# Three edits to a fused attention and gated-FFN kernel: row transposes on the DMA, a swapped subtraction, and a nested product in the paired FFN blocks

## The chip, the cores and the metric

The kernel runs on one core of one Trainium2 chip. The metric is device time in microseconds (us) from launch to end. A core has five engines with a queue each: TensorE (PE, matrix products), VectorE (DVE), ScalarE (ACT), GpSimd (POOL) and SyncE (SP, which here issues most DMAs). Each engine works through its own queue in order and waits for others by semaphores. TensorE writes its results to PSUM, which has eight banks of 128 x 512 fp32 values.

## The reference

```python
h  = x + _A_ref(_layernorm(x), wqkv, wo)      # x: 1 x 2048 x 1024, bf16
h2 = h + _B_ref(_layernorm(h), w_gate, w_up, w_down)

def _A_ref(x, wqkv, wo):      # 32 heads of 32, each position looks at itself
    ...                       # and 7 earlier ones, 2 apart
    return softmax-weighted values @ wo

def _B_ref(x, w_gate, w_up, w_down):          # F = 3584
    g = jnp.einsum("bsd,df->bsf", x, w_gate)
    u = jnp.einsum("bsd,df->bsf", x, w_up)
    return jnp.einsum("bsf,fd->bsd", g * u, w_down)
```

Both layer norms have mean and variance over 1024 values, without weights.

## The kernel before, in words

The 2048 rows are worked on in four chunks of 512 (0 to 3). A chunk's rows are normalized and transposed, so that `lnT` holds 8 slices of 128 features by 512 rows. Projections follow, in groups of eight matmuls of 512 columns that fill a PSUM bank (line 489); then attention on VectorE, the output projection `wo`, a second normalization, and the FFN. All instructions are emitted in a schedule written by hand: each engine executes its part in the order in which the program emits it. A `Background` object slips VectorE and ScalarE work (attention, normalization) in between the groups, according to a budget in us that the generators state with `yield`.

*Chunk 1's first normalization.* `rows_gen` (lines 249 to 262) emits, for four row tiles of 128 rows, statistics (`stat`), the normalized rows (`norm`, line 195) and the transpose. Tiles 0 and 1 are transposed on TensorE (line 245: eight 128 x 128 transposes a tile, into two PSUM banks) and copied to `lnT` by ScalarE and VectorE (line 247). Tiles 2 and 3 are transposed by a DMA issued from ScalarE's queue (line 236). Chunk 2 uses the same generator without transposes. Chunk 1's tile is first multiplied after the twelve groups of chunk 0's blocks 1 to 3. SyncE's queue meanwhile stores queries (line 395) and keys and values (line 415), and loads weights (line 172) and rows (line 209).

*The FFN of chunks 0 and 1* is done group by group. *Chunks 2 and 3* are worked on together, with sums in the manner of Strassen and Winograd: a product of 2 x 2 blocks takes seven block products instead of eight. Here the two halves of the 1024 features and the two chunks make the activation blocks `b11` to `b22`; two halves of a weight tile of 256 columns and two halves of the features make the weight blocks. `activation_sums` (line 835) makes the differences `t1` to `t4` once. There are 14 blocks (`NP`), each for 256 columns of both `w_gate` (i = 0) and `w_up` (i = 1). `weight_sums(n)` scales block n's weights to fp16 (line 823, VectorE) and makes four sums of 128 x 512 for gate and for up (lines 828 to 831), on VectorE for block 0 and on GpSimd for the others; it is emitted at the start of block n-1, so it runs while TensorE works on block n-1. GpSimd does gate's four sums first, then up's.

`pair_block(n)` (line 850) has fourteen products of four matmuls of 512 columns (line 847, `product`), seven for gate and seven for up, in banks x, y, z and v. A partial result is copied from bank to bank by ScalarE (lines 864 and 872) and further products are added to the copy. The fifth product of each (bank v, `sw[:, i, 0]` by `t1`) goes to SBUF scaled, as `p5` (line 869), and is added by VectorE to two of the four outputs (lines 875 and 884). Outputs of gate and up are then multiplied (line 886). Earlier outputs are summed by their absolute values on ScalarE (line 369, `sums`). PSUM tiles share one pool of eight buffers, and a block uses eight.

*Chunk 1's down projection* runs before the paired blocks, likewise in seven products (`dprod`, line 1108; `t_half`, line 1101, for differences of the weights; `put`, line 805, for results). Its last part is interleaved with the second normalization of chunk 3: after `rstd_of` on ScalarE, VectorE forms the bias `nbs[3]` (line 1351), which ScalarE uses for the rows (`ln_rows`, line 1197). Line 1352 and line 1354 form `t4` in two halves, from `b21` (loaded and converted before) and `t2`.

Of the kernel before, what the change touches and what calls it, by code (L numbers as in the profile page):

```python
# [25 lines left out]
TC = 512  # L26
NCH = S // TC
SUB = TC // 4
KO = D // 128
NF = F // 128  # L30
NP = NF // 2
# [47 lines left out]
def kernel(  # L79
# [11 lines left out]
    nc = tc.nc  # L91
    x = A_x.flatten_outer_dims()
# [7 lines left out]
    lnTp = ctx.enter_context(tc.tile_pool(name="lnT", bufs=3))  # L100
# [4 lines left out]
    att = ctx.enter_context(tc.tile_pool(name="att", bufs=1))  # L105
    psum = ctx.enter_context(tc.tile_pool(name="psum", bufs=8, space=PSUM))
# [106 lines left out]
    lnTs = {}  # L213
# [3 lines left out]
    class Norm1:  # L217
# [11 lines left out]
        def norm(self, t):  # L229
            self.lns[t] = normalize(xtiles[self.c][t], self.mv4, self.rs4, t)  # L230

        def transpose(self, t, eng=nc.sync):
            c = self.c
            if c not in lnTs:
                lnTs[c] = lnTp.tile([128, KO, TC], BF, tag="lnT", name=f"lnT1_{c}")
            eng.dma_start_transpose(lnTs[c][:, :, bass.ts(t, 128)], self.lns[t][:])

        def transpose_on_array(self, t):
            c = self.c
            if c not in lnTs:  # L240
                lnTs[c] = lnTp.tile([128, KO, TC], BF, tag="lnT", name=f"lnT1_{c}")
            for hf in range(2):
                pt = psum.tile([128, KO // 2, 128], BF, tag="mm", name=f"ptb{c}_{t}_{hf}")
                for kk in range(KO // 2):
                    nc.tensor.transpose(pt[:, kk, :], self.lns[t][:, bass.ts(4 * hf + kk, 128)], ident[:])
                copy = nc.vector.tensor_copy if hf else nc.scalar.copy
                copy(lnTs[c][:, bass.ts(hf, 4), bass.ts(t, 128)], pt[:])

    def rows_gen(n, on_array):
        for t in range(6):  # L250
            if t < 4:
                n.stat(t)
                yield 1.5
            if 0 < t < 5:
                n.norm(t - 1)
                yield 0.55
            if t > 1 and on_array:
                if t < 4:
                    n.transpose_on_array(t - 2)
                    yield 0.45  # L260
                else:
                    n.transpose(t - 2, nc.scalar)

    class NormOnScalar(Norm1):

# [80 lines left out]
    ident = const.tile([128, 128], BF)  # L346
# [131 lines left out]
    xtiles[2] = load_x(2, "x", nc.sync)  # L478
    norm1 = {1: Norm1(1), 2: Norm1(2), 3: NormOnScalar(3)}
    bg.add(rows_gen(norm1[1], True))  # L480
    rows2 = rows_gen(norm1[2], False)
    bg.add(rows2)
    for j in range(4):
# [324 lines left out]
    pair = {}  # L808
# [8 lines left out]
    def weight_sums(n, eng=nc.gpsimd):  # L817
        raw = pair["w", n]
        wt = wpool.tile([128, KO, 2, 256], F16, tag="w", name=f"ws_{n}")
        if n == 0:  # L820
            nc.scalar.activation(wt[:], raw[:], ACTF.Copy, scale=scale_gu.s)
        else:
            nc.vector.tensor_scalar(wt[:], raw[:], scale_gu.s, None, ALU.mult)
        sw = wpool.tile([128, 2, 4, 4, 128], F16, tag="w", name=f"sw_{n}")
        for i in ((slice(0, 2),) if eng is nc.vector else (slice(0, 1), slice(1, 2))):
            a11, a21, a12, a22 = (wt[:, k:k + 4, i, c:c + 128].rearrange("p k i c -> p i k c")
                                  for k in (0, 4) for c in (0, 128))
            eng.tensor_tensor(sw[:, i, 0], a21, a22, ALU.add)  # L828
            eng.tensor_tensor(sw[:, i, 1], sw[:, i, 0], a11, ALU.subtract)  # L829
            eng.tensor_tensor(sw[:, i, 2], a11, a21, ALU.subtract)  # L830
            eng.tensor_tensor(sw[:, i, 3], a12, sw[:, i, 1], ALU.subtract)  # L831
        pair["a", n], pair["s", n] = wt, sw
        state["live"] += 1

# [10 lines left out]
    def product(ps, lhs, rhs, fresh):  # L845
        for ko in range(4):
            nc.tensor.matmul(ps[:], lhsT=lhs[:, ko, :], rhs=rhs[:, ko, :], start=(fresh and ko == 0),  # L847
                             stop=(ko == 3), skip_group_check=not fresh)

    def pair_block(n, hts, sums=()):  # L850
        b11, b21, t1, t2, t3, t4, b22 = pair["b"]
        wt, sw, inv = pair["a", n], pair["s", n], scale_gu.inv
        gu = range(2)
        out = [hts, [t1k.tile([128, TC], BF, tag="t1k", name=f"up{n}_{k}")[:] for k in range(4)]]

        def bank(k, i):
            return psum.tile([128, TC], F32, tag="mm", name=f"p{k}{n}_{i}")

        xb, yb, zb, vb, p5 = [[None] * 2 for _ in range(5)]
        for i in gu:  # L860
            xb[i] = bank("x", i)
            product(xb[i], wt[:, 0:4, i, 0:128], b11, True)
            yb[i] = bank("y", i)
            nc.scalar.copy(yb[i][:], xb[i][:])  # L864
        for i in gu:
            vb[i] = bank("v", i)
            product(vb[i], sw[:, i, 0], t1, True)
            p5[i] = att.tile([128, TC], F32, tag=("lg", "t3")[i], name=f"p5{n}_{i}")
            nc.scalar.activation(p5[i][:], vb[i][:], ACTF.Copy, scale=inv)
            product(yb[i], sw[:, i, 1], t2, False)  # L870
            zb[i] = bank("z", i)
            nc.scalar.copy(zb[i][:], yb[i][:])
        for i in gu:
            product(zb[i], sw[:, i, 2], t3, False)
            nc.vector.scalar_tensor_tensor(out[i][3], zb[i][:], inv, p5[i][:], ALU.mult, ALU.add)
            product(xb[i], wt[:, 4:8, i, 0:128], b21, False)
            nc.scalar.activation(out[i][0], xb[i][:], ACTF.Copy, scale=inv)
            for k in sums[2 * i:2 * i + 2]:
                k()
        for i in gu:  # L880
            product(zb[i], wt[:, 4:8, i, 128:256], t4, False)
            nc.scalar.activation(out[i][2], zb[i][:], ACTF.Copy, scale=inv)
            product(yb[i], sw[:, i, 3], b22, False)
            nc.vector.scalar_tensor_tensor(out[i][1], yb[i][:], inv, p5[i][:], ALU.mult, ALU.add)
        for k in (3, 0, 2, 1):
            nc.vector.tensor_tensor(out[0][k], out[0][k], out[1][k], ALU.mult)
        state["live"] -= 2
# [211 lines left out]
    def sub(dst, x0, x1, eng=nc.vector):  # L1099
        for d, a0, a1 in zip(dst, x0, x1):  # L1100
            eng.tensor_tensor(f16(d[:, 0:NH, :]), f16(a0[:, 0:NH, :]), f16(a1[:, 0:NH, :]), ALU.subtract)
# [25 lines left out]
    b11, b21 = ([wts["dn", n, a] for a in range(2)] for n in ("11", "21"))  # L1127

    def halves(parts, name):
        return [pool.tile([128, KO, TC], BF, tag=tag, name=f"{name}{i}") for i, (pool, tag) in enumerate(parts)]  # L1130

    b12 = halves(((att, "qD"), (att, "kD")), "b12")
    a21 = halves(((lnTp, "lnT"), (lnTp, "lnT")), "a21")
    a22 = halves(((lnTp, "lnT"), (wpool, "w")), "a22")
# [33 lines left out]
    def ln_stat(c, t):  # L1168
        stats(hss[c][t], ln2[c][0], t)
# [42 lines left out]
    def t_half(dst, x0, x1, a):  # L1212
        sub([dst[a]], [x0[a]], [x1[a]])
# [42 lines left out]
    b22 = halves(((lnTp, "lnT"), (wpool, "w")), "b22")  # L1256
# [15 lines left out]
    t2 = halves(((wpool, "w"), (wpool, "w")), "t2_")  # L1272
# [16 lines left out]
    room = wpool.tile([128, 4, TC], F32, tag="w", name="hsr0")  # L1289
# [4 lines left out]
    b21 = halves(((lnTp, "lnT"), (lnTp, "lnT")), "b21r")  # L1294
# [10 lines left out]
    a22 = halves(((att, "vD"), (att, "oD")), "a22r")  # L1305
# [42 lines left out]
    t4 = t2  # L1348
    ln_stat(3, 3)
    rstd_of(ln2[3][0], ln2[3][1], 0, 4)  # L1350
    nc.vector.scalar_tensor_tensor(nbs[3], ln2[3][0][:, :, 0], -1.0, ln2[3][1][:], ALU.mult, ALU.mult)
    t_half(t4, b21, t2, 0)
    l3 = lnTp.tile([128, KO, TC], BF, tag="lnT", name="lnT2_3")
    t_half(t4, b21, t2, 1)
    for q in range(4):
# [4 lines left out]
    retire(2)  # L1360
    load_pair(1)
    weight_sums(0, nc.vector)
    for q in range(4):
        dprod(zs[q], q, F22, fcells(t4), False)
# [153 lines left out]
```

## Time and profile before

| | |
|---|---|
| median of 10 runs | 767.84 us (767.62 to 768.65) |
| the profiled execution | 768.01 us, span of its instructions 765.9 us |
| granted TensorE clock | 1.000 |
| matmul instructions | 3648 |
| matmuls of the paired blocks (line 847) | 784 of 512 columns |
| line 836 to 842, `activation_sums` | four VectorE operations of 1.2 us |
| DMA | 145.77 MB, mean 190 GB/s |

The span runs from the first to the last instruction; the time of an execution has some 2 us around it. In lines of operations the columns are: start in us, duration in us, engine, line, operation, tile written <- tiles read, shapes, count, and in brackets how long the engine had been idle before and what ended that. In rows of a line's statistics, three durations are the shortest, the median and the longest in ns. Rows of several operations ("x3") give the time from the first start to the last end. The row of a stretch gives its bounds, its length, and the busy us of PE, the weight loads (PEld), DVE, ACT and POOL, each with a number of instructions, then the clock, the DMA share and GB/s. A wait row gives total us, number of times, and the longest.

### The profile page before, as it was taken

Reading aid. Unit: us, or ns where it says so; the run is one execution under the profiler, and the core shown is the slowest. Engines: PE = TensorE matmul, PEld = TensorE weight load, DVE = VectorE, ACT = ScalarE, POOL = GpSimd, SP = SyncE. Lnnn points to the kernel's source line nnn. Section 1 sums busy time; section 2 is a strip of 40 time slices with the busy share of each in tenths; the row PEclk is TensorE's granted clock in tenths of the full one; section 3 lists DMA queues with packets and bytes.
Section 4 is the critical chain, followed back from the end, with each engine's and each line's share of the span. In section 5 each row is a group of like instructions: output and inputs, shape, how many; then the busy total and the mean of one; then the engine's idle time right before and its main releaser. Section 6 shows DMA issues by size and latency. Waiting matters only on the chain.

```text
span 765.9 us, 10355 instructions
## 1 busy us (share of the span) xinstructions
PE 759.6 (99%) x3648; PEld 349.3 (46%) x3648; DVE 627.8 (82%) x760; ACT 532.9 (70%) x1012; POOL 144.7 (19%) x155
## 2 busy tenths in 40 slices
PE   8999999999999999999999999999999999999998
PEld 5444444444444444444444444444444444444444
DVE  6789999999999999999999999976554454578862
ACT  4757854556799598996898984846767677788230
POOL 0010000200001000010000001018778777600000
PEclk9999999999999999999999999999999999999999
DMA  8889794968998959869768528684242432830001
GB/s 270 232 236 262 183 288 106 321 176 193 326 342 285 312 168 316 259 229 339 251 213 280 171 92 285 147 203 127 63 110 58 108 90 76 269 117 27 1 28 55
DMA packets 191987, 145.77 MB, mean 190 GB/s; under 512 B 81856, under 2 KB 182080, under 8 KB 189888
## 3 DMA queue, kind: packets, MB, share of 16 engines
q1 hardware_dynamic: 180416, 116.94, 53.6%
q0 software_dynamic: 3728, 22.02, 8.4%
q10 hardware_dynamic: 7792, 6.16, 2.7%
q8 instruction: 28, 0.46, 0.3%
q14 instruction: 23, 0.19, 0.1%
HBM read 111.02 MB, written 27.26 MB: 181 GB/s over the span
## 4 chain that ended last, share of the span: by engine, by line
PE 86%; DVE 5%; ACT 5%; DMA 3%; issue 0%; SPq 0%; ACTq 0%; DVEq 0%
PE ps L489 17%; PE dx L1108 6%; PE py L847 6%; PE px L847 6%; PE pwg L489 6%; PE pz L847 6%; PE pwu L489 6%; PE pu L489 6%; PE pg L489 6%; PE wo L661 4%; PE pv L847 3%; PE dy L1108 3%; PE wo L1162 2%; DMA b21r<-in_B_w_down_dram 2%; PE ez L1108 2%; ACT gs L1087 1%
## 5 line engine op out<-in xcount | busy, mean ns | idle before, releaser
L489 PE MATMUL ps<-lnT,w_qkv 128*128 128x512 bf16 x608 | 132.1, 379 | 0.0
L489 PEld LDWEIGHTS <-w_qkv 128*128 128x128 bf16 (+1 forms) x608 | 59.3, 98 | 70.9
L546 DVE TENSOR_TENSOR prod<-qD,kD 128x4096 bf16<-128x4096 bf16 (+1 forms) x34 | 72.2, 2158 | 2.2 <-DMA kD<-kd 2.2
L594 DVE TENSOR_TENSOR pv<-vD,at 128x4096 bf16<-128x4096 bf16 x32 | 72.4, 2286 | 0.3
L847 PEld LDWEIGHTS <-sw 128*128 128x128 f16 x448 | 43.8, 98 | 52.9 <-issue 0.2
L489 PEld LDWEIGHTS <-w_wg 128*128 128x128 bf16 x448 | 43.8, 98 | 52.8
L489 PEld LDWEIGHTS <-w_wu 128*128 128x128 bf16 x448 | 43.8, 98 | 52.9
L403 ACT CAST sg<-ps 128x512 bf16<-128x512 f32 x72 | 41.5, 584 | 31.9 <-PE ps L489 27.3
L847 PE MATMUL px<-lnT,ws 128*128 128x512 bf16 x224 | 55.2, 379 | 0.0
L489 PE MATMUL pg<-lnT,w_wg 128*128 128x512 bf16 x224 | 52.9, 379 | 0.0
L489 PE MATMUL pu<-lnT,w_wu 128*128 128x512 bf16 x224 | 52.9, 379 | 0.0
L489 PE MATMUL pwu<-lnT,w_wu 128*128 128x512 bf16 x224 | 52.9, 379 | 0.0
L489 PE MATMUL pwg<-lnT,w_wg 128*128 128x512 bf16 x224 | 52.9, 379 | 0.0
L847 PEld LDWEIGHTS <-ws 128*128 128x128 f16 x336 | 32.9, 98 | 39.7
L607 POOL DMA_DIRECT2D od<-oD x4 | 2.2, 542 | 250.1 <-DVE oD L605 250.1
L828 POOL TENSOR_TENSOR sw<-ws 128x512 f16<-128x512 f16 x26 | 30.0, 1153 | 79.0 <-PE pz L847 47.4
L1108 PEld LDWEIGHTS <-gs 128*128 128x128 f16 (+1 forms) x280 | 27.3, 98 | 33.1 <-DVE gs L1276 0.5
L548 DVE TENSOR_TENSOR prod<-prod 128x4096 bf16<-128x4096 bf16 x16 | 36.6, 2286 | 0.3
L864 ACT COPY py<-px 128x512 f32<-128x512 f32 x28 | 16.0, 570 | 24.4 <-PE px L847 24.4
L831 POOL TENSOR_TENSOR sw<-ws,sw 128x512 f16<-128x512 f16 x26 | 30.6, 1175 | 0.0
L829 POOL TENSOR_TENSOR sw<-sw,ws 128x512 f16<-128x512 f16 x26 | 30.0, 1153 | 2.0
L830 POOL TENSOR_TENSOR sw<-ws 128x512 f16<-128x512 f16 x26 | 30.2, 1160 | 0.0
(371 smaller groups left out, 1577.8 us busy)
## 6 DMA issues: line engine op xcount, KB each, us to landing
w_wg<-in_B_w_gate_dram SPq DMA_DIRECT2D x14, 1024.0 KB, 7.5
w_wu<-in_B_w_up_dram SPq DMA_DIRECT2D x14, 1024.0 KB, 9.3
w_pair<-in_B_w_gate_dram SPq DMA_DIRECT2D x14, 512.0 KB, 4.0
w_pair<-in_B_w_up_dram SPq DMA_DIRECT2D x14, 512.0 KB, 5.3
w_wo<-in_A_wo_dram SPq DMA_DIRECT2D x6, 1024.0 KB, 8.3
w_qkv<-in_A_wqkv_dram SPq DMA_DIRECT2D x5, 1024.0 KB, 9.3
kd<-sg SPq DMA_DIRECT2D x32, 144.0 KB, 4.2
vd<-sg SPq DMA_DIRECT2D x32, 144.0 KB, 3.2
```

The costliest lines, as they stand in the source:

```text
L403: nc.scalar.copy(sg[:, HB:HB + TC], ps[:])
L489: nc.tensor.matmul(ps[:], lhsT=wt[:, ko, bass.ts(j, 128)], rhs=rhs[:, ko, :], start=(ko == 0), stop=(ko == KO - 1))
L546: nc.vector.tensor_tensor(prod[:, j, ds], qD[:, ds], kD[:, ds, o:o + SUB], ALU.mult)
L548: nc.vector.tensor_tensor(prod[:, :, 0:16], prod[:, :, 0:16], prod[:, :, 16:32], ALU.add)
L594: nc.vector.tensor_tensor(pv[:, j], vD[:, :, o:o + SUB], at[:, w, None, :].to_broadcast((128, DH, SUB)), ALU.mult)
L661: nc.tensor.matmul(ps[:], lhsT=oTs[c][:, kk, t, :], rhs=wts["wo", c, hf][:, kk, :], start=(kk == 0), stop=(kk == KO - 1))
L828: eng.tensor_tensor(sw[:, i, 0], a21, a22, ALU.add)
L829: eng.tensor_tensor(sw[:, i, 1], sw[:, i, 0], a11, ALU.subtract)
L830: eng.tensor_tensor(sw[:, i, 2], a11, a21, ALU.subtract)
L831: eng.tensor_tensor(sw[:, i, 3], a12, sw[:, i, 1], ALU.subtract)
L847: nc.tensor.matmul(ps[:], lhsT=lhs[:, ko, :], rhs=rhs[:, ko, :], start=(fresh and ko == 0), stop=(ko == 3), skip_group_check=not fresh)
L1108: nc.tensor.matmul(ps[:, bass.ds(lo, n)], lhsT=lhs[k][:, bass.ts(q, 128)], rhs=rhs[k][:, bass.ds(lo, n)], start=(fresh and k == 0), stop=( ...
```

## The change

Chunk 1: all four row tiles are transposed by DMA from SyncE's queue; the method that used TensorE is gone, with its copies and the 0.45 that the generator charged for each.

```diff
-        def transpose(self, t, eng=nc.sync):
+        def transpose(self, t):
...
-            eng.dma_start_transpose(lnTs[c][:, :, bass.ts(t, 128)], self.lns[t][:])
-
-        def transpose_on_array(self, t):
...
+            nc.sync.dma_start_transpose(lnTs[c][:, :, bass.ts(t, 128)], self.lns[t][:])
...
-            if t > 1 and on_array:
-                if t < 4:
-                    n.transpose_on_array(t - 2)
-                    yield 0.45
-                else:
-                    n.transpose(t - 2, nc.scalar)
+            if t > 1 and turned:
+                n.transpose(t - 2)
```

Chunk 1's down weights: the first half of `t4` is emitted ahead of the bias.

```diff
     rstd_of(ln2[3][0], ln2[3][1], 0, 4)
+    t_half(t4, b21, t2, 0)
     nc.vector.scalar_tensor_tensor(nbs[3], ln2[3][0][:, :, 0], -1.0, ln2[3][1][:], ALU.mult, ALU.mult)
-    t_half(t4, b21, t2, 0)
```

The paired blocks: in blocks 1 to 13 the two fifth products (gate's and up's, together 256 columns of weights by 512 features by 512 values of `t1`) are taken as one product of 2 x 2 blocks and done again in seven smaller products, `inner`, each two matmuls of 256 columns. Two banks, `first` and `last`, take the place of the two banks v. `inner_rows` makes the differences of `t1` once, in block 0; `inner_weights(n + 1)` makes the weights' sums in every block but the last, on VectorE between the two operations of line 884. GpSimd's sums are emitted one kind at a time, for gate and up, in place of all kinds for gate and then for up.

```diff
-        for i in ((slice(0, 2),) if eng is nc.vector else (slice(0, 1), slice(1, 2))):
...
+        for j, x, y, op in ((0, a21, a22, ALU.add), (1, sw[:, :, 0], a11, ALU.subtract), (2, a11, a21, ALU.subtract),
+                            (3, a12, sw[:, :, 1], ALU.subtract)):
+            for i in each:
+                eng.tensor_tensor(sw[:, i, j], x[:, i], y[:, i], op)
...
+    def inner_rows(t):
+        room = att.tile([128, KO, TC], F16, tag="vD", name="inner_t")
+        b11, b12, b21, b22 = (t[:, k:k + 2, c:c + 256] for k in (0, 2) for c in (0, 256))
+        t1, t2, t3, t4 = (room[:, i, :].rearrange("p (k c) -> p k c", k=2) for i in range(4))
+        nc.vector.tensor_tensor(t1, b12, b11, ALU.subtract)
+        nc.vector.tensor_tensor(t2, b22, t1, ALU.subtract)
+        nc.vector.tensor_tensor(t3, b22, b12, ALU.subtract)
+        nc.vector.tensor_tensor(t4, b21, t2, ALU.subtract)
+        pair["iv"] = room[:, 4, :].bitcast(F32)
+        pair["ib"] = (b11, b21, t1, t2, t3, t4, b22)
+
+    def inner_weights(n):
+        sw = pair["s", n]
+        a11, a12, a21, a22 = (sw[:, i, 0, k:k + 2, :] for i in range(2) for k in (0, 2))
+        room = att.tile([128, 4, 2, 128], F16, tag="at", name=f"inner_w{n}")
+        s1, s2, s3, s4 = (room[:, i] for i in range(4))
+        nc.vector.tensor_tensor(s1, a21, a22, ALU.add)
+        nc.vector.tensor_tensor(s2, s1, a11, ALU.subtract)
+        nc.vector.tensor_tensor(s3, a11, a21, ALU.subtract)
+        nc.vector.tensor_tensor(s4, a12, s2, ALU.subtract)
+        pair["ia", n] = (a11, a12, a22, s1, s2, s3, s4)
+
+    def inner(ps, lhs, rhs, fresh):
+        for k in range(2):
+            nc.tensor.matmul(ps, lhsT=lhs[:, k, :], rhs=rhs[:, k, :], start=(fresh and k == 0), stop=(k == 1),
+                             skip_group_check=not fresh)
...
+            first, last = bank("i", 0), bank("i", 1)
+            lx, lv = (first[:, bass.ts(i, 256)] for i in range(2))
+            ly, lz = (last[:, bass.ts(i, 256)] for i in range(2))
+            v5 = pair["iv"]
         for i in gu:
...
             nc.scalar.copy(yb[i][:], xb[i][:])
+            if nested and i == 0:
+                inner(lx, a11, c11, True)
+                inner(lv, s1, r1, False)
+                nc.scalar.activation(v5, lv, ACTF.Copy, scale=inv)
+                nc.scalar.copy(ly, lx)
         for i in gu:
-            vb[i] = bank("v", i)
-            product(vb[i], sw[:, i, 0], t1, True)
...
+            if not nested:
+                vb[i] = bank("v", i)
+                product(vb[i], sw[:, i, 0], t1, True)
+                nc.scalar.activation(p5[i][:], vb[i][:], ACTF.Copy, scale=inv)
             product(yb[i], sw[:, i, 1], t2, False)
...
+            if nested and i == 0:
+                inner(ly, s2, r2, False)
+                inner(lx, a12, c21, False)
+                nc.scalar.copy(lz, ly)
+                nc.scalar.activation(p5[0][:, 0:256], lx, ACTF.Copy, scale=inv)
+        if nested:
+            inner(lz, s3, r3, False)
+            inner(ly, s4, c22, False)
+            nc.vector.scalar_tensor_tensor(p5[0][:, 256:512], ly, inv, v5, ALU.mult, ALU.add)
+            nc.vector.scalar_tensor_tensor(p5[1][:, 256:512], lz, inv, v5, ALU.mult, ALU.add)
         for i in gu:
...
             nc.scalar.activation(out[i][0], xb[i][:], ACTF.Copy, scale=inv)
+            if nested and i == 0:
+                inner(lz, a22, r4, False)
+                nc.scalar.activation(p5[1][:, 0:256], lz, ACTF.Copy, scale=inv)
...
             nc.vector.scalar_tensor_tensor(out[i][1], yb[i][:], inv, p5[i][:], ALU.mult, ALU.add)
+            if i == 0 and n + 1 < NP:
+                if n == 0:
+                    inner_rows(t1)
+                inner_weights(n + 1)
```

More of the change, by code (lines that the diff above doesn't have):

```diff
@@ L235, in transpose, with rows_gen @@
                 lnTs[c] = lnTp.tile([128, KO, TC], BF, tag="lnT", name=f"lnT1_{c}")
-            eng.dma_start_transpose(lnTs[c][:, :, bass.ts(t, 128)], self.lns[t][:])
-        def transpose_on_array(self, t):
[L239 to L249, printed above, removed]
+            nc.sync.dma_start_transpose(lnTs[c][:, :, bass.ts(t, 128)], self.lns[t][:])
+    def rows_gen(n, turned):
         for t in range(6):
@@ L824, in weight_sums @@
         sw = wpool.tile([128, 2, 4, 4, 128], F16, tag="w", name=f"sw_{n}")
-        for i in ((slice(0, 2),) if eng is nc.vector else (slice(0, 1), slice(1, 2))):
[L826 to L831, printed above, removed]
+        a11, a21, a12, a22 = (wt[:, k:k + 4, :, c:c + 128].rearrange("p k i c -> p i k c")
+                              for k in (0, 4) for c in (0, 128))
+        both = (slice(0, 2),)
+        each = both if eng is nc.vector else (slice(0, 1), slice(1, 2))
+        for j, x, y, op in ((0, a21, a22, ALU.add), (1, sw[:, :, 0], a11, ALU.subtract), (2, a11, a21, ALU.subtract),
+                            (3, a12, sw[:, :, 1], ALU.subtract)):
+            for i in each:
+                eng.tensor_tensor(sw[:, i, j], x[:, i], y[:, i], op)
         pair["a", n], pair["s", n] = wt, sw
@@ L859, in pair_block @@
         xb, yb, zb, vb, p5 = [[None] * 2 for _ in range(5)]
+        nested = ("ia", n) in pair
+        if nested:
+            a11, a12, a22, s1, s2, s3, s4 = pair["ia", n]
+            c11, c21, r1, r2, r3, r4, c22 = pair["ib"]
+            first, last = bank("i", 0), bank("i", 1)
+            lx, lv = (first[:, bass.ts(i, 256)] for i in range(2))
+            ly, lz = (last[:, bass.ts(i, 256)] for i in range(2))
+            v5 = pair["iv"]
         for i in gu:
+            p5[i] = att.tile([128, TC], F32, tag=("lg", "t3")[i], name=f"p5{n}_{i}")
             xb[i] = bank("x", i)
@@ L864, in pair_block @@
             nc.scalar.copy(yb[i][:], xb[i][:])
+            if nested and i == 0:
[3 more added lines that the diff above has]
+                nc.scalar.copy(ly, lx)
         for i in gu:
-            vb[i] = bank("v", i)
-            product(vb[i], sw[:, i, 0], t1, True)
-            p5[i] = att.tile([128, TC], F32, tag=("lg", "t3")[i], name=f"p5{n}_{i}")
-            nc.scalar.activation(p5[i][:], vb[i][:], ACTF.Copy, scale=inv)
+            if not nested:
+                vb[i] = bank("v", i)
+                product(vb[i], sw[:, i, 0], t1, True)
+                nc.scalar.activation(p5[i][:], vb[i][:], ACTF.Copy, scale=inv)
             product(yb[i], sw[:, i, 1], t2, False)
@@ L872, in pair_block @@
             nc.scalar.copy(zb[i][:], yb[i][:])
+            if nested and i == 0:
[3 more added lines that the diff above has]
+                nc.scalar.activation(p5[0][:, 0:256], lx, ACTF.Copy, scale=inv)
+        if nested:
+            inner(lz, s3, r3, False)
+            inner(ly, s4, c22, False)
+            nc.vector.scalar_tensor_tensor(p5[0][:, 256:512], ly, inv, v5, ALU.mult, ALU.add)
+            nc.vector.scalar_tensor_tensor(p5[1][:, 256:512], lz, inv, v5, ALU.mult, ALU.add)
         for i in gu:
```

## The prediction

> **What bounds the kernel now.** I read the page's engine totals first, then what TensorE waited for, then the stretch of the paired blocks (508 to 677 us), then the order of time inside single blocks.
>
> ```profile
> PE 759.6 (99%) x3648; PEld 349.3 (46%) x3648; DVE 627.8 (82%) x760; ACT 532.9 (70%) x1012; POOL 144.7 (19%) x155
> ...
> PE ez L1108 <- DVE hsr L805: 0.3, 1, 0.3
> ...
> 508.23:677.35 169.12, 169.12 (x785) 76.61 (x783) 87.88 (x127) 118.44 (x244) 117.92 (x104) 1.00 0.39 112
> ```
>
> TensorE has no gap: after the start its longest wait is 0.3 us at line 1108, and in the 14 paired blocks it is busy for all 169.12 us, 12.08 a block. So time taken off TensorE shortens the kernel, and any new wait of TensorE lengthens it. GpSimd's 117.92 us in that stretch look like slack; whether they are depends on VectorE:
>
> ```profile
> 518.96 1.16 POOL L828 TENSOR_TENSOR sw<-ws 128x512 f16<-128x512 f16 x1
> 520.20 1.15 POOL L829 TENSOR_TENSOR sw<-sw,ws 128x512 f16<-128x512 f16 x1
> 520.43 0.75 DVE L884 SCALAR_TENSOR_TENSOR up<-py,ibgu,p 128x512 bf16<-128x512 f32 x1 [0.98 <-PE py L847]
> 521.10 3.12 DVE L886 TENSOR_TENSOR hq<-hq,up 128x512 bf16<-128x512 bf16 x3
> 521.31 1.33 POOL L830 TENSOR_TENSOR sw<-ws 128x512 f16<-128x512 f16 x1
> 522.60 1.33 POOL L831 TENSOR_TENSOR sw<-ws,sw 128x512 f16<-128x512 f16 x1
> ...
> 654.05 1.42 DVE L886 TENSOR_TENSOR hq_l<-hq_l,up 128x512 bf16<-128x512 bf16 x4
> 655.39 1.28 DVE L823 TENSOR_SCALAR ws<-w_pair,sbgu 128x4096 f16<-128x4096 bf16 x1
> 656.80 1.15 POOL L828 TENSOR_TENSOR sw<-ws 128x512 f16<-128x512 f16 x1 [2.92 <-PE py L847]
> ...
> 664.82 1.16 POOL L831 TENSOR_TENSOR sw<-ws,sw 128x512 f16<-128x512 f16 x1
> 665.27 1.89 PE L847 MATMUL px<-lnT,ws 128*128 128x512 bf16 x8
> ...
> L886 DVE TENSOR_TENSOR hq<-hq,up x24: 410/412/1372, 521.1 to 582.9; 128x512 bf16<-128x512 bf16 x24
> L831 POOL TENSOR_TENSOR sw<-ws,sw x26: 1147/1155/1341, 517.9 to 664.8; 128x512 f16<-128x512 f16 x26
> ```
>
> Four products of line 886 take 1.42 us when GpSimd is idle (654.05); three take 3.12 while it works (521.10), one of them up to 1.372 instead of 0.41, and the GpSimd operations between them stretch from 1.15 to 1.33. So a VectorE operation with two SBUF inputs waits for the GpSimd operation in progress, and they take turns: one VectorE operation for each GpSimd operation, about 1.2 us a turn. Line 884 and 875, which read PSUM, stay at 0.75. GpSimd's eight operations for the next block run from 656.80 to 665.98, that is, from 3.6 to 12.8 us after the start (653.18) of a 12.08 us block.
>
> **What the Trainium skill says.** "SBUF — State Buffer", section "SBUF: two separate sides": VectorE and GpSimd share one port pair under an exclusive lock, taken by a VectorE operation with two SBUF inputs against a GpSimd operation that reads SBUF; the loser "fully blocks". The trace agrees (1.372 against 0.41). "TensorE: Matmul & The Clock Gate", "Back-to-back issue gap": N/2.4 + 2.5 ns. The trace agrees for 512 columns (12.085 / 56 = 215.8 ns) and 384 (six in 0.98 us, 163 ns), as the first starts here show:
>
> ```profile
> 759.40 1.14 PE L1108 MATMUL dy<-dn_b22a,hq 128*128 128x384 f16 x6
> 760.38 0.33 PE L1108 MATMUL dy<-dn_b22a,hq_q 128*128 128x384 f16 x1
> ...
> 24.32 0.61 PE L245 MATMUL ptb<-ident,ln 128*128 128x128 bf16 x8
> 24.77 1.89 PE L489 MATMUL ps<-lnT,w_qkv 128*128 128x512 bf16 x8
> 26.50 0.61 PE L245 MATMUL ptb<-ident,ln 128*128 128x128 bf16 x8
> 26.94 8.80 PE L489 MATMUL ps<-lnT,w_qkv 128*128 128x512 bf16 x40
> ```
>
> **Part A, chunk 1's transposes.** Sixteen transposes leave TensorE: 0.45 + 0.44 us (24.32 to 24.77, 26.50 to 26.94), 0.89 of pure path, with four copies (line 247) on ScalarE and VectorE. ScalarE also loses two DMA issues of 2.77 us. SyncE gains four issues of about 1.29 us (median of line 236), landing 3.2 us later. TensorE wants the whole of chunk 1's tile at 17.42 + 12 x 1.73 = 38.2. The rows are normalized by 28.0, so the last transpose is issued near 30 and lands near 34; queued behind them on SyncE are stores of queries and keys, and the last keys of chunk 0 are stored only at about 42. Bound on the bad side: on this queue at 55 us four such issues took 11.34 us behind a backlog of loads; from 24.5 that ends at 35.9, lands at 39.1, and costs 1 us. I take -0.89; ends -0.9 and +0.1.
>
> **Part B, the swapped subtraction.** VectorE sat 1.00 us before line 1351 (the bias, 490.44) waiting for ScalarE, with both 1.97 us subtractions of line 1101 behind it; TensorE then waited 0.26 us at 495.98. The first subtraction's inputs are converted at 485.5, so it fills that wait. The bias comes about 1 us later, and so do the rows of line 1197; ScalarE's 4.0 us idle before line 821 covers that. -0.26; ends -0.3 and 0.
>
> **Part C, the nested product.** Removed in each of 13 blocks: eight matmuls of 512 columns, 8 x 0.2158 = 1.726 us. Added: fourteen of 256 columns at 0.109 (an estimate from the formula above, between the rows for 128 and 384) = 1.526. Gain 0.20 a block, 2.6 in all, if nothing waits. ScalarE loses two operations of 0.69 and gains five of half the width, at 0.36 to 0.47 (the page "ScalarE: Activation LUTs", "What ACT_TABLE_LOAD costs", gives 0.833 ns an element; 512 columns took 0.57 and 0.69): +0.85 on some 9 busy us in 12, and each copy is ready at least 0.2 us before TensorE's product.
>
> VectorE is where it fails. It gains two half-width PSUM operations (about 0.48, unlocked) and four additions of two SBUF inputs (the next block's inner weights), placed between the two operations of line 884. There VectorE idled 0.97 us; alone the four need some 0.9. But GpSimd is then at work until 12.8, so they take turns with it. Behind them in VectorE's queue stand the second operation of line 884 (which frees bank y1), the four products of line 886, and line 823, which starts GpSimd's next batch. Let E be the end of the four. Then:
> - line 884 reads y1 until E + 0.75; ScalarE's copy into y1 of the next block (0.57) ends at E + 1.32, and TensorE's product on y1 starts at E + 1.36. From there to the end of the product on y0 are seven products and three inner ones, 7 x 0.863 + 3 x 0.218 = 6.70; 0.2 of latency and 0.67 of line 884 later VectorE comes to the next four: E + 8.93.
> - line 886 (4 x 0.34) and line 823 (1.28) after line 884 (0.67) start GpSimd at about E + 3.4; eight operations at 1.11 end at E + 12.3.
>
> So GpSimd has 3.4 us left when the four begin: three turns and one free operation, W = 3.9 us. A block lasts 8.93 + 3.9 = 12.85, against 11.885 unstalled; I take 12.9. It cannot settle lower: GpSimd's batch (8.9), the chain of line 884, 886 and 823 (3.4) and the additions' own tail exceed 11.885, so a small wait grows from block to block. Ends for W: 3.4 (no tail) and 4.6 (four full turns), 12.3 to 13.5 a block.
>
> Block 0 starts it. After its first line 884 (518.70 + 0.67) VectorE has four row differences of 512 columns and the four weights; GpSimd runs until 523.9, so the rows take four turns, the weights 0.9 more, and line 884 ends near 525.6 instead of 521.2. Eight banks in rotation put block 1's y0 on block 0's y1: ScalarE's copy ends at 526.2, and TensorE, due at 522.5, waits 3.7. Block 1 lasts 15.6. Putting operations of one kind first on GpSimd only makes the needed sums early; its batch keeps its length.
>
> Sum: 12.1 + 15.6 + 12 x 12.9 = 182.5 against 169.1, +13.4. With A and B: +12.2. The profiled execution took 768.01 us (span 765.9 and 2.1 around it), 0.17 above the median 767.84. Forecast 780.2.
>
> **Rivals.**
> - No lock for these: the added operations are narrow and could slip between GpSimd's. Then only block 1 waits, 0.4 us (eight operations of 0.2 to 0.35): 768.0 - 1.15 - 2.6 + 0.4 = 764.7, faster. For it: half the bytes. Against it: the turns in the trace are per operation, not per byte. It decides if W stays below 2.9, the value at which 8.93 + W equals 11.885.
> - Turns, but no growth: W settles below 2.9 because VectorE finishes the chain sooner than I sum. Block 1's 3.7 stays: 768.0 - 1.15 - 2.6 + 3.7 = 768.0, no change.
> - Transposes late on SyncE: 1 us more on any of these, and later loads behind them; 781.2 with the first.
>
> **How the numbers follow.** Chances: my case 0.74 (with late transposes or a longer batch 0.77 in all slower), no lock 0.15, turns without growth 0.08 (about half of it no change, the rest mostly faster). A single measurement here tells 0.2% (1.5 us) from nothing. The slow case alone spans 773 to 787.5 (W from 3.4 to 4.6, block 1 give or take 1 us). The range reaches down to 767 to take in the rival without growth; left out are the case without the lock and little above. Faster 0.18, same 0.05, slower 0.77.
>
> **What would show it.** Right: additions of 256 columns on VectorE at about 1.2 us each, GpSimd operations at 1.2, blocks of 12.9 us, TensorE waiting in each block for the product on y1, ScalarE's copy before it waiting for VectorE's line 884, one wait of 3 to 4 us in block 1. Also no wait where chunk 1 begins, and none at 495. Wrong: additions at 0.3, blocks of 11.9, TensorE idle nowhere. Inner matmuls spaced by more than 0.125 us would undo the 0.20 without any wait.

## The result, and the profile after

The changed kernel takes 775.47 us (median of 8 runs, 775.06 to 776.0) against 767.95 of the kernel before (28 runs): a ratio of 1.0097, 95% interval 1.0088 to 1.0106, or 7.5 us slower. Its profiled execution took 775.2 us with a span of 773.4, which is 7.5 over the span before.

The page's engine totals, and then what TensorE waited for (total us, times, longest):

```profile
PE 758.6 (98%) x3710; PEld 356.1 (46%) x3710; DVE 679.9 (88%) x840; ACT 538.4 (70%) x1049; POOL 145.0 (19%) x155
```

```profile
PE pi L860 <- DVE p L910: 6.8, 11, 1.4
PE pi L860 <- DVE inner_w L852: 2.9, 1, 2.9
```

TensorE is busy 1.0 us less than before, although 62 matmul records came on top; GpSimd is the same. But there are twelve new waits, all at line 860 (the inner products) and all for VectorE: one for the first inner weight (line 852), eleven for the two half-width operations that read the inner results (lines 909 and 910). The wait at the old line 1108 is gone. The stretch of the paired blocks in the same columns as before:

```profile
506.61:684.92 178.31, 168.70 (x863) 84.19 (x862) 140.68 (x209) 125.05 (x283) 118.43 (x104) 1.00 0.38 108
```

Between the same two instructions, the first product and the first `dx`, the kernel before took 677.35 - 508.07 = 169.28. So the stretch is 9.03 longer; it starts 1.46 earlier (506.61 against 508.07), and what follows it is 0.07 shorter: 9.03 - 1.46 - 0.07 = 7.5. VectorE's busy time in it went from 87.88 to 140.68 us, time in which its operations are held up by GpSimd included.

Line numbers below are those of the changed kernel: 833 is `product` (847 before), 860 `inner`, 925 the operations of line 884, 931 those of 886, 808 the scaling of 823, 817 GpSimd's last sum.

Block 0 to block 1, in order of time (columns as in the rows before; only some are shown):

```profile
517.91 0.83 DVE L840 TENSOR_TENSOR inner_t<-prodx 128x512 f16<-128x512 f16 x1
...
519.89 0.57 ACT L886 COPY py<-px 128x512 f32<-128x512 f32 x1 [1.09 <-PE px L833]
...
521.25 1.36 DVE L843 TENSOR_TENSOR inner_t<-prodx,inner_t 128x512 f16<-128x512 f16 x1
522.54 0.28 DVE L852 TENSOR_TENSOR inner_w<-sw 128x256 f16<-128x256 f16 x1
...
522.88 0.39 PE L860 MATMUL pi<-inner_t,inner_w 128*128 128x256 f16 x2 [2.86 <-DVE inner_w L852]
...
523.47 0.74 DVE L925 SCALAR_TENSOR_TENSOR up<-py,ibgu,p 128x512 bf16<-128x512 f32 x1
```

The four row differences (840 to 843) take turns with GpSimd, up to 1.36 us each in these rows; the first inner weight stands behind them, and TensorE stands behind it, idle for 2.86 us. ScalarE's copy into block 1's first bank y starts at 519.89, 3.6 us before VectorE reads block 0's last bank y (523.47). It waits for a product, not for VectorE: these two are not the same bank.

A later block, first from the order of time (again only some rows) and then from the chain that ended last:

```profile
645.45 0.51 DVE L852 TENSOR_TENSOR inner_w<-sw 128x256 f16<-128x256 f16 x1
646.00 1.12 DVE L853 TENSOR_TENSOR inner_w<-inner_w,sw 128x256 f16<-128x256 f16 x1
646.94 2.35 POOL L817 TENSOR_TENSOR sw<-ws,sw 128x512 f16<-128x512 f16 x2
647.05 1.23 DVE L854 TENSOR_TENSOR inner_w<-sw 128x256 f16<-128x256 f16 x1
648.20 1.24 DVE L855 TENSOR_TENSOR inner_w<-sw,inner_w 128x256 f16<-128x256 f16 x1
...
648.67 0.57 ACT L886 COPY py<-px 128x512 f32<-128x512 f32 x1
...
649.36 0.74 DVE L925 SCALAR_TENSOR_TENSOR up<-py,ibgu,p 128x512 bf16<-128x512 f32 x1
```

```profile
645.54 0.44 DVE inner_w L852
...
646.00 1.12 DVE inner_w L853
647.12 1.16 DVE inner_w L854
648.28 1.16 DVE inner_w L855
649.44 0.66 DVE up L925
...
650.36 0.94 DVE hq_l L931 x3
...
651.36 1.27 DVE ws L808
652.64 0.39 DVE p L909
653.03 0.40 DVE p L910
...
653.47 0.38 PE pi L860 x2
...
657.34 0.75 DVE hq_l L925
```

In the first view, the second copy into the next block's banks y starts at 648.67, 0.69 us before line 925 reads the old block's last bank y (649.36); here too ScalarE does not wait for VectorE. The second view is the whole loop of one block. From the first inner addition to the second operation of line 925 there are 3.90 us (three turns and one short operation). From there VectorE's own queue goes on: line 925, four products (931), the scaling (808), then lines 909 and 910. Only then may TensorE add the seventh inner product to the bank that 910 has read (653.47), four products of 0.86 us later VectorE is at line 925 again, and its end is 8.65 us after 649.44. 3.90 + 8.65 = 12.55 a block, where TensorE alone needs 11.89 (measured below).

The first copies of successive blocks (line 886) start at 519.89, 534.81, 546.76, 559.40, 572.05 and then about every 12.56 us. A block's first product starts 1.1 us ahead of its first copy, so the last block, from its copy at 672.55 to the first `dx` at 684.92, lasts 13.5. Against 11.89, block 1 loses 3.0, block 2 0.1, blocks 3 to 12 about 0.69 each, and the last 1.6 (a conversion of down weights stands there ahead of line 909): 11.6 in all, of which the waits show 9.7 as idle. The difference, 0.16 us a wait, fits the way in which idle time is counted: the record of a matmul of 512 columns lasts 0.379 us, but where nothing waits the next one starts 0.216 us after it, and a wait is counted only from the record's end.

### The profile page after: what moved, and what is told of

The parts are those of the page before. It is cut to its first block, busy times and chain, and to the rows that moved or that the text cites. A ratio compares the mean times of both kernels' runs of the same rounds, so it can differ in the third digit from the quotient of the medians.

```text
span 773.4 us, 10621 instructions
## 1 busy us (share of the span) xinstructions
PE 758.6 (98%) x3710; PEld 356.1 (46%) x3710; DVE 679.9 (88%) x840; ACT 538.4 (70%) x1049; POOL 145.0 (19%) x155
## 5 line engine op out<-in xcount | busy, mean ns | idle before, releaser
L833 PE MATMUL px<-lnT,ws 128*128 128x512 bf16 x224 | 57.3, 379 | 0.0
L833 PEld LDWEIGHTS <-sw 128*128 128x128 f16 x344 | 33.6, 98 | 32.4 <-issue 0.2
L833 PE MATMUL py<-prodx,sw 128*128 128x512 f16 x112 | 28.7, 379 | 0.0
```

## The experiments

All times are medians, with the ratio to the kernel before on the same chip. Two theories stood against each other once the trace was read: the turns delay lines 909 and 910, for which the seventh inner product waits; or the turns delay line 925's reading of bank y1, as the prediction had it.

**The parts by themselves.** First the kernel before with the transposes and the swap alone:

```diff
-            if t > 1 and on_array:
...
+            if t > 1 and turned:
+                n.transpose(t - 2)
...
+    t_half(t4, b21, t2, 0)
     nc.vector.scalar_tensor_tensor(nbs[3], ln2[3][0][:, :, 0], -1.0, ln2[3][1][:], ALU.mult, ALU.mult)
-    t_half(t4, b21, t2, 0)
```

> The kernel before with the transposes and the swapped subtraction alone, paired blocks as before. My theory (TensorE is the bound outside the paired blocks, so its sixteen transposes and its 0.26 us wait come off the end): 1.1 to 1.3 us less than before, 766.7. Rival (the DMA transposes on SyncE hold up stores and loads and give part of it back): 768 or more.

Measured: 766.28 us, 0.9976 (0.9968 to 0.9985). Then the other half, the changed kernel with these lines put back:

```diff
+            if t > 1 and on_array:
...
-            if t > 1 and turned:
-                n.transpose(t - 2)
...
-    t_half(t4, b21, t2, 0)
     nc.vector.scalar_tensor_tensor(nbs[3], ln2[3][0][:, :, 0], -1.0, ln2[3][1][:], ALU.mult, ALU.mult)
+    t_half(t4, b21, t2, 0)
```

> The nested product alone, with chunk 1's transposes and the order of the bias as before. If the parts add: 7.5 + 1.2 = 8.7 us more than before, 776.6, with the paired blocks as in the changed kernel. Rival (the earlier edits shifted the phase in which the blocks start and the loss depends on that): any other number.

Measured: 776.78, 1.0114 (1.0101 to 1.0128), with the same two waits (6.7 us in 11, and 3.1 once). The whole loss belongs to the nested product; the two other edits gain.

The first two edits one by one, in the kernel before. The transposes:

```diff
-            if t > 1 and on_array:
...
+            if t > 1 and turned:
+                n.transpose(t - 2)
```

> Chunk 1's transposes by DMA from SyncE alone. Prediction on record: 0.89 us less (the sixteen transposes of TensorE), and the wait of 0.26 us at the subtraction stays in the trace: 767.1. Both early edits together measured 1.7 us less, with 1.2 explained; if the transposes alone give more than 0.9, something else moved.

and the swap:

```diff
+    t_half(t4, b21, t2, 0)
     nc.vector.scalar_tensor_tensor(nbs[3], ln2[3][0][:, :, 0], -1.0, ln2[3][1][:], ALU.mult, ALU.mult)
-    t_half(t4, b21, t2, 0)
```

> The swapped subtraction alone: TensorE's wait at the last part of chunk 1's down projection is gone from the trace, 0.26 us less, which the times can hardly tell from nothing: 767.7.

Measured: 767.13, 0.9989 (0.9983 to 0.9996), and 767.51, 0.9992 (0.9984 to 1.0). The wait of 0.3 at the old line 1108 stays with the transposes alone and is gone with the swap alone. The swap's interval touches no change.

**Weights made, not used.** The additions of lines 840 to 843 and 852 to 855 stay, and the products are those of before; the result is complete.

```diff
-        nested = ("ia", n) in pair
+        nested = False
```

> The changed kernel in which the inner rows and weights are made at their places, but the fifth products are those of before and nothing reads the inner weights: the result is the full one. The additions take turns with GpSimd (about 1.15 us each), but TensorE waits for no operation of VectorE behind line 808 in the same block: no wait of TensorE, 766 to 767, as with the two early edits alone. Theory on record (bank y1): the late line 925 holds up ScalarE's copy and TensorE, 778 or more. Rival (the lock does nothing): additions of 0.28, 766.

Measured: 766.47, 0.9981 (0.9974 to 0.9989), level with the first experiment's 766.28. The statistics of line 855 (count, shortest, median and longest ns) and the longest wait of TensorE in this kernel:

```profile
L855 DVE TENSOR_TENSOR inner_w<-sw,inner_w x13: 284/1236/1239, 523.0 to 666.5; 128x256 f16<-128x256 f16 x13
```

```profile
PE warm_ps L342 <- DVE warm L328: 1.2, 1, 1.2
```

The additions still take up to 1.24 us each, and TensorE waits nowhere after the start (line 342 is the warming up). So turns on VectorE cost nothing as long as no instruction of TensorE needs what stands behind them. On the theory of bank y1 the time of this kernel decides little, because without nesting the product on y1 comes later: in a block of this trace it starts at 644.23, and a copy held back until line 925 had read old y1 (643.01 to 643.75) would have been ready about then. What speaks against that theory are the copies themselves: the two into the next block's banks y start at 641.03 and 641.90, ahead of the reading, as in the changed kernel.

**The seventh inner product later**, behind up's product on bank z, so that lines 909 and 910 get one product, 0.86 us, more time (the expectation counted two, 1.73):

```diff
             product(zb[i], sw[:, i, 2], t3, False)
+            if nested and i == 1:
+                inner(lz, a22, r4, False)
+                nc.scalar.activation(p5[1][:, 0:256], lz, ACTF.Copy, scale=inv)
             nc.vector.scalar_tensor_tensor(out[i][3], zb[i][:], inv, p5[i][:], ALU.mult, ALU.add)
...
-            if nested and i == 0:
-                inner(lz, a22, r4, False)
-                nc.scalar.activation(p5[1][:, 0:256], lz, ACTF.Copy, scale=inv)
```

> The changed kernel with the seventh inner product (bank lz) and its copy moved behind the product on z of the up half, 1.73 us of TensorE later; GpSimd as in the changed kernel. Read from the changed kernel's chain, a block is closed by VectorE's line 910, which the seventh inner product waits for: then the loop shortens by 1.73 to 10.8 us plus waits, below TensorE's own 11.885, while the turns with GpSimd stay at four, perhaps 0.6 us longer: blocks of 11.9 to 12.3 us, 768 to 772. Theory on record (bank y1 closes the loop): no change, 775.5.

Measured: 771.65, 1.0047 (1.0032 to 1.0062), 3.8 us less than the changed kernel. The waits for line 910 fall from 6.8 us to 2.5; the copies at line 886 show that blocks alternate late in the stretch, one of 12.45 us and one of 11.89. That moving this one instruction moves the time shows that the wait sits in it. Block 1's wait (3.1) is still there, and this profile shows something more behind it:

```profile
523.12 0.60 PE L860 MATMUL pi<-inner_t,inner_w 128*128 128x256 f16 x2 [3.07 <-DVE inner_w L852]
523.51 1.91 PE L833 MATMUL px<-lnT,ws 128*128 128x512 bf16 x4
525.22 1.70 PE L833 MATMUL py<-prodx,sw 128*128 128x512 f16 x4
```

After the wait, four matmuls of 512 columns take 1.71 us from start to start where they take 0.86 elsewhere: TensorE's granted clock was 0.57 on average from 523 to 527 us. Block 1 lasts 16.82 us instead of 14.92. So some 1.7 us of this execution are the clock's (523.12 to 526.76 takes 3.64 us, at the usual spacing 1.95). The old order of GpSimd (below) shows the same after a wait of 3.23; the profiles of the changed kernel (2.86) and of the nested product alone (3.09) do not. The mean clock of an execution is 0.997 or 0.998 in all four executions of this kernel, which the dip would account for, and 0.998 in four of the eight of the changed kernel, which took 0.5 us longer on average than the other four.

**Row differences earlier.** In block 0 they are emitted behind the last operation of line 913, ahead of line 925:

```diff
             nc.vector.scalar_tensor_tensor(out[i][3], zb[i][:], inv, p5[i][:], ALU.mult, ALU.add)
+            if i == 1 and n == 0:
+                inner_rows(t1)
...
-                if n == 0:
-                    inner_rows(t1)
```

> The changed kernel with the four differences of t1's rows made earlier in block 0, behind line 913 of the up half, not between the two operations of line 925. They still take turns with GpSimd, but the inner weights of block 1 come earlier. If the wait of 2.86 us in block 1 comes from the rows' turns, 1.5 to 2.8 us of it go and the other blocks stay at 12.57: 773 to 774. Rival (the wait moves into the next blocks, since they settle at the same loop anyway): 775.5.

Measured: 774.29, 1.0083 (1.0068 to 1.0098), just above the 773 to 774 expected. The wait for line 852 goes from 2.9 to 1.0, but only 1.2 us come of it: the wait for line 910 now begins one block sooner (12 times, 7.2 us in all).

**GpSimd in the old order**, gate's four sums first. The sums are the same and so is their length:

```diff
-            for i in each:
-                eng.tensor_tensor(sw[:, i, j], x[:, i], y[:, i], op)
+        for i in ((slice(0, 2),) if eng is nc.vector else (slice(0, 1), slice(1, 2))):
...
+            eng.tensor_tensor(sw[:, i, 0], a21, a22, ALU.add)
+            eng.tensor_tensor(sw[:, i, 1], sw[:, i, 0], a11, ALU.subtract)
...
```

> The changed kernel with GpSimd's sums in the order of before: the four of gate, then the four of up. The inner weights then need GpSimd's fifth operation in place of its second. GpSimd starts 5.3 us before them and an operation takes 1.1 to 1.2, so the fifth is done about when they begin: 775.5 to 777. If it is 780 or more, the new order was needed.

Measured: 779.08, 1.0144 (1.0127 to 1.0161): a miss, 2 us above what was expected. From this kernel's order of time (its lines are one lower, and 813 is the first kind of sum):

```profile
622.49 1.15 POOL L813 TENSOR_TENSOR sw<-ws 128x512 f16<-128x512 f16 x1
...
623.67 0.29 DVE L851 TENSOR_TENSOR inner_w<-sw 128x256 f16<-128x256 f16 x1 [0.42 <-POOL sw L813]
```

The first inner addition needs up's first sum, which in this order is GpSimd's fifth; it ends 0.42 us after VectorE is free. Then three more operations of GpSimd are still to come, and so three full turns. A block lasts 631.48 - 618.63 = 12.85 instead of 12.56, and the loop runs through GpSimd as well. The order of the sums, which the prediction gave no weight, is worth 3.6 us here (3.7 between the medians of the executions whose mean clock is 1.000, so it is not the slower clock that block 1 of this profile shows).

**All sums on VectorE**, at the place where GpSimd's were emitted (the start of the block), so that nothing is left to take turns with:

```diff
-            weight_sums(n + 1)
+            weight_sums(n + 1, nc.vector)
```

> The changed kernel with the sums of the weights on VectorE as in the fastest run, but emitted at the block's start, behind line 808 and ahead of lines 909 and 910; the rows' differences stay where the change has them. No turns: additions of 0.28. But line 910 now stands behind 2.4 us of sums: 0.9 + 1.3 + 1.2 + 2.5 + 0.8 = 6.7 us after the block's start, when the inner product on lz is due at 6.5: about 0.2 to 0.4 us of wait a block and 1 us in block 1, 767 to 769. If work on VectorE were what costs, and not the turns, this is 776 or more.

Measured: 771.67, 1.0046 (1.0032 to 1.006); a miss in size. The turns are gone (the inner additions take 280 to 293 ns), yet TensorE waits for line 910 in 12 of the 13 nested blocks, 5.3 us in sum: 1.66 in block 1 and 0.33 in each of the others. The 0.33 is within the 0.2 to 0.4 expected, but a block gets 0.49 longer by it, since idle time leaves out 0.16. The chain of this kernel:

```profile
623.37 0.76 DVE sw L817 x2
...
624.58 0.68 DVE sw L817
625.26 0.40 DVE p L909
625.66 0.40 DVE p L910
...
626.10 0.38 PE pi L860 x2
```

Four sums of 0.7 us stand in VectorE's queue ahead of lines 909 and 910. A block lasts 626.10 - 613.72 = 12.38. So it is not the lock by itself that stalls TensorE, but whatever puts lines 909 and 910 late.

**All sums on VectorE, in the middle of the block**, behind gate's operation of line 913, where lines 909 and 910 are done (`mid()` emits the four sums of block n + 1, each for gate and up together); the row differences in block 0 behind up's:

```diff
             nc.vector.scalar_tensor_tensor(out[i][3], zb[i][:], inv, p5[i][:], ALU.mult, ALU.add)
+            if i == 0 and mid:
+                mid()
+            if i == 1 and n == 0:
+                inner_rows(t1)
...
-            weight_sums(n + 1)
+            mid = weight_sums(n + 1, True)
```

> The changed kernel with all sums of the weights on VectorE, in the middle of a block, and the differences of the rows of t1 made earlier in block 0; GpSimd does no arithmetic in the paired blocks. Lock theory: the four inner additions take 0.28 each, nobody waits, blocks take 11.9 us, 764.2. Rival (VectorE has too much to do, the lock matters little): VectorE gains 2.4 us of sums in each block, so blocks get longer than 12.57 and the time rises above 776.

and the same without the nested product (every block in the form of before, no inner weights):

> As the run with all sums on VectorE in the middle of a block, but without nesting: the fifth products as before, no inner weights. Both theories: blocks of 12.08 us, so the time of the kernel with the two early edits alone, 766.7. The difference to the nested one is the worth of the nesting itself: 13 x 0.2 = 2.6 us.

Measured: 764.04, 0.9945 (0.9933 to 0.9958), and 766.27, 0.9975 (0.9964 to 0.9985). The first is the fastest of all, 3.9 us below the kernel before and 11.4 below the changed one. A block of it on VectorE, and the stretch of the paired blocks:

```profile
643.82 0.68 DVE L815 TENSOR_TENSOR sw<-ws 128x1024 f16<-128x1024 f16 x1
...
648.30 0.28 DVE L854 TENSOR_TENSOR inner_w<-sw 128x256 f16<-128x256 f16 x1
...
654.19 0.48 DVE L911 SCALAR_TENSOR_TENSOR p<-pi,ibgu,inner_t 128x256 f32<-128x256 f32 x1 [1.54 <-PE pi L862]
```

```profile
506.23:672.94 166.71, 166.71 (x864) 84.35 (x863) 136.64 (x262) 121.28 (x283) 0.00 (x0) 1.00 0.41 116
```

The inner additions take 0.28 us, VectorE waits 1.54 us for TensorE where in the changed kernel TensorE waited for VectorE, and TensorE is busy for the whole 166.71 us, 11.89 a block with nesting. VectorE is busy for 136.64 us in the stretch, four less than in the changed kernel, with GpSimd's 118.43 us of work added to it: a sum of twice the size takes 0.68 us on VectorE, and 2 x 1.15 on GpSimd.

Without nesting the stretch lasts from 506.88 to 676.17, 169.29. So nesting, when nothing waits, gains 2.58 us in 13 blocks, 0.198 a block; and moving the sums to VectorE gains nothing by itself (766.27 against 766.28), since TensorE did not wait for GpSimd before.

## Why the prediction was right, and where it was off

*Direction, and the cause as far as VectorE.* Right: slower was forecast, at 780.2, and 775.47 was measured. The inner additions take turns with GpSimd, one operation for one: 1.12 to 1.24 us instead of 0.28, W = 3.90 against the 3.9 predicted. The rival without a lock needed additions near 0.3; the rival without growth needed W below 2.9. That the turns are what delays VectorE is shown by the pair of kernels with sums in the middle of the block; that the delay matters only by way of the nested products is shown by the kernel with unused weights.

*The step that failed* is the loop that the prediction closed by way of bank y1: "ScalarE's copy into y1 of the next block (0.57) ends at E + 1.32, and TensorE's product on y1 starts at E + 1.36 ... VectorE comes to the next four: E + 8.93". The copy did not wait for VectorE at all (519.89 ahead of 523.47, and 648.67 ahead of 649.36). So the next block's banks y were not old y1, and counting out eight banks in rotation was wrong. Two signs that the prediction named, TensorE waiting for the product on y1 and ScalarE's copy waiting for VectorE, did not come. In its place stands a longer way along VectorE's queue, from line 925 through 931, 808, 909 to 910, and then the seventh inner product: E + 8.65. It was in view: the prediction listed lines 931 and 808 as standing behind the additions, and put "two half-width PSUM operations" down as a cost of 0.48 each without asking where they stand in the queue and who waits for them. That it comes out within 0.3 us of E + 8.93 is chance, and it is why the size of a block (12.55 against 12.85) looked nearly right.

The floor that the prediction set under a block ("It cannot settle lower", from GpSimd's batch, the chain to line 823 and the tail of the additions, 12.3 us and more) did not hold as such either. In the kernel with unused weights the same batch and the same chain fit in a block of 12.09 us (copies at 641.03 and 653.12): there the additions end at 643.09, 1.0 us before GpSimd's last operation (644.10), while in the changed kernel they end with it (649.44 and 649.29).

*The sizes.* The paired blocks cost 9.03 and not 13.4. The prediction's sum for the stretch was 182.5, and 178.3 was measured. The terms: blocks 3 to 12 take 12.58 on average and not 12.9, 3.2 less; block 2 takes 11.95, 0.95 less, most likely because VectorE had caught up while TensorE waited in block 1; block 1 takes 14.92 and not 15.6, 0.7 less; and the last block takes 0.6 more, with the conversion of down weights ahead of line 909. "One wait of 3 to 4 us in block 1" was 2.86, and it was for the first inner weight, not for a bank. For ScalarE's half-width operations, the 0.36 to 0.47 us is an estimate from the 0.833 ns an element of the Trainium skill, page "ScalarE: Activation LUTs", section "What ACT_TABLE_LOAD costs", and the length of whole ones; they took 0.36 to 0.49 in the changed kernel.

*Gain of nesting itself.* Right: 0.198 a block against 0.20, from 256 columns at 0.109 us. The Trainium skill, page "TensorE: Matmul & The Clock Gate", section "Back-to-back issue gap", gives N/2.4 + 2.5 ns, for a matmul by itself; at 256 columns that is 109.2 ns, and in the stream here two inner matmuls take 0.22 us from start to start of the next pair. For a stream of weight loads and matmuls the same section gives about 131 ns at 512 columns; here such a stream took 215.8.

*Transposes.* -0.89 was taken; alone they bring 0.95 (768.08 - 767.13). The way there was less comfortable than stated:

```profile
17.28 17.43 PE L474 MATMUL ps<-lnT,w_qkv 128*128 128x512 bf16 x80
...
28.40 1.33 SPq L236 DMA_TRANSPOSE lnT<-ln  x1
29.83 0.52 SPq L400 DMA_DIRECT2D kd<-sg  x1
30.44 4.02 SPq L236 DMA_TRANSPOSE lnT<-ln  x3
```

In the changed kernel's order of time, SyncE's queue was storing queries until 28.3, so the first transpose was issued at 28.4 and the last at about 33.2, not "near 30"; it landed near 36.7, and TensorE, at work without a break on 80 matmuls from 17.28, wants the tile at about 38. The stores of queries ahead of it were left out of the prediction's estimate; 1.3 us were left.

*The swap.* -0.26 was taken; the wait is gone, and alone it brings 0.57 with an interval that reaches to nothing. In the profiles the products behind the old wait start 12.08 us after the group ahead of them (482.44 and 494.52), before 12.50 (483.48 and 495.98): 0.42 less, the 0.26 of idle time and the 0.16 that idle time leaves out. So -0.26 was too small by that. The bias came 0.8 us later, near the 1 us predicted, counted from the last statistics ahead of it (488.20 to 490.21, before 489.23 to 490.44); the first subtraction began at 488.32 and filled time that VectorE had idled. Together the two edits gave 1.7, where the two alone sum to 1.5; these runs can't tell the two figures apart.

*Left open.* Why, with the seventh inner product moved, every second block still waits, and why the turns there do not settle at one length, was not followed up. Nor do these runs say what decides whether a wait of some 3 us is followed by the slower clock.

## What to carry to other kernels

- If an instruction is delayed on an engine that isn't the bound, go through everything that stands behind it in that engine's queue, and for each ask who waits for it. The loop that sets the time is the longest of these, and it can run through a small instruction that costs 0.4 us.
- A delay is harmless until something on the bounding engine needs what stands behind it: the same turns cost 0 us (weights unused) or 9 us (weights used). Placing the work where the queue has no waiter behind it, here in the middle of the block after lines 909 and 910, is worth more than making it faster: the kernel with the same sums on VectorE took 771.67 us with them at the start of the block and 764.04 with them in the middle (the row differences of block 0 stand elsewhere in the two as well; at most block 1's wait of 1.66 us can be due to them).
- Where two engines contend for SBUF, give the whole stream to one of them if it has the room: twice the width took 0.68 us on VectorE and 2.3 us on GpSimd.

## What the runs showed of the hardware that was not expected

- The price of a turn between VectorE and GpSimd is per operation and not per byte. An addition of 256 columns took 1.12 to 1.24 us in turns and 0.28 without; one of 512 columns up to 1.37. GpSimd's operations had one size throughout, so their own width was not tested. The Trainium skill, page "SBUF — State Buffer", section "SBUF: two separate sides", describes an exclusive lock that blocks the loser fully, and the traces agree: the length of a turn is that of GpSimd's operation, 1.15 to 1.2 us.
- The order in which GpSimd makes its sums, with their number and size unchanged, was worth 3.6 us: what VectorE needs first must not stand fifth.
- A wait of TensorE lengthens the time by some 0.16 us more than its idle time says: 9.7 us of waits against 11.6 us of lengthened blocks, about the 0.379 us of a record less the 0.216 from start to start. The same sum gives 0.17 in the kernels with the nested product alone, with the rows earlier, and with all sums at the start.
- After waits of 3.07 and 3.23 us TensorE ran at about half its speed for some 3 us (0.43 us from one matmul of 512 columns to the next instead of 0.216; the granted clock was 0.57 on average from 523 to 527 us in both profiles). After waits of 2.86 and 3.09 us in two other kernels it did not.
